# Backward attention of a decode block: dV made up to eight heads ahead of dK, and the matmuls of dq spread over the fronts

## The chip, the cores and the metric

The kernel runs on one core of a Trainium2 chip. The metric is the device time of one launch in microseconds; the number given for a kernel is the median of several runs. Five engines work side by side, each with a queue of its own that it takes in order: TensorE (PE), VectorE (DVE), ScalarE (ACT), GpSimd (POOL) and SyncE (SP). SP does no arithmetic here; it issues nearly all transfers between HBM and the memory on the chip (SBUF). The transfers themselves run on 16 DMA engines that the core's queues share.

## The reference

One layer of a decoder for one new token per sequence (batch B = 4), forward and backward. There are H = 32 heads of width Dh = 128 over a cache of Sk = 4096 positions:

```python
q = (x_ln @ wq).reshape(B, 1, H, Dh).transpose(0, 2, 1, 3)
p = softmax(einsum("bhqd,bhkd->bhqk", q, k_cache) * Dh ** -0.5)
o = einsum("bhqk,bhkd->bhqd", p, v_cache)
h = x + o.reshape(B, 1, H * Dh) @ wo
out = h + swiglu(layernorm(h), w1, w3, w2)
# returned: out, and the gradients of x, k_cache, v_cache, wq, wo, w1, w3, w2
```

All is bfloat16. For each of the 128 pairs of sequence and head, called heads here and counted by s, the backward part needs dP = V dO, dS = P (dP − c) scale with c = dO·O, and the outer products dV = P dOᵀ and dK = dS qᵀ. A head's K, V, dK or dV is 4096 × 128 values, 1024 KB. So K is read once, V twice, dK and dV are written once: 128 MB for each of the five streams.

## The kernel before, in words

The order of every engine's queue is the order in which the program writes the instructions; there is no scheduler. What an instruction waits for follows from the tiles that it reads and writes.

**Memory.** 23 slots of 8 KB per partition (class `Slot`) hold everything large: a head of K, V, dK or dV, a piece of a weight matrix, or 16 of the matrices M. `give()` puts a slot at the back of a list, and the next request takes the front of it; an instruction that writes to a slot waits until the work that last used it has ended, transfers included. V's second reading uses a ring of its own (`vring`) of seven slots once the first heads are through.

**Forward part.** It streams K and V by pairs of heads, makes the softmax and, for each head, M = Vᵀ [P K, P] on TensorE (slots `Ms`, eight of them, 16 heads each), whose columns later give dq. Then comes a middle part (the `with ExitStack() as cm` block): the gated MLP forward and backward, the gradient dh at the attention's output, and the first eight columns of heads of dO (`dO_columns(0, 8, ...)`, L907 to L940). V loads for the backward part (L797) are issued as slots come free. dV of heads 0 and 1 are made here already.

**Backward part.** Its pieces are functions:

- `front(s)` turns V of a head: four groups of eight transposes on TensorE (L764), each copied back over V by ScalarE (L765); then eight matmuls with dO as stationary operand (L1177) add dP of four heads into one PSUM tile. The stationary operand is a window of 32 columns into one of four zero-padded tiles `zd`, in which `dO_window(s)` puts the column of dO (GpSimd, L1142). `front(s)` fills the window of head s + 2. Then V's slot goes back to the ring, and `load_ahead` and `prefetch` issue the next V load into it from SP.
- `rows_out` and `rows_T` copy the finished dP of four heads out and turn it (L1152, L1159), inside the next group's first front; `group_dS` makes dS of the four heads on VectorE (L1191, L1194).
- `P_pairs(s)` lays each value of P down twice (GpSimd, L1147, three buffers); `replicate(i0)` spreads four rows of dO and of q over all partitions (TensorE L1128, ScalarE L1131).
- `grad_V(s)` and `grad_K(s)` make an outer product each on VectorE (L770) into a fresh slot, and SP stores it (L781, L1201).

Ahead of the loop, fronts 0 to 4 are written, with dV of heads 2 and 3 behind fronts 2 and 3; then `group_dS(0)`. In the loop, round s writes `front(s + 5)`, `grad_V(s + 3)`, `grad_K(s)`:

```python
        O0, S0, L, LV = 2, 21, 5, 3
```

Two generators are advanced step by step in the rounds: `rest_of_dO`, unit "o", from round 2 to 20 (the other 24 heads of dO in pages of eight, with the transposes of wo), and `side_work`, unit "s", from round 21, three steps a round for 15 rounds and two after. `side_work` begins with dq: one fp32 matmul a head (L964), three heads a step, which releases a slot of M after each 16 heads; then dx, the gradients of wq, w2, w1, w3 and wo.

Of the kernel before, what the change touches and what calls it, by code (L numbers as in the profile page):

```python
# [9 lines left out]
FP32 = mybir.dt.float32  # L10
BF16 = mybir.dt.bfloat16
# [13 lines left out]
def kernel(  # L25
# [22 lines left out]
    nc = tc.nc  # L48
    P = nc.NUM_PARTITIONS

    B = A_x.shape[0]
# [3 lines left out]
    Dh = A_k_cache.shape[3]  # L55
    F = B_w1.shape[1]
    NH = B * H
    HD = H * Dh
    assert NH == P and Dh == P and H == 32 and Sk == 32 * P
    assert D == 4 * P and F % P == 0  # L60
    DC = D // P
# [5 lines left out]
    MC = 16  # L67
# [3 lines left out]
    x2 = A_x.rearrange("b s d -> (b s) d")  # L71
# [91 lines left out]
    ident_b = const.tile([P, P], BF16, name="ident_b")  # L163
# [14 lines left out]
    def ones_window(col):  # L178
# [11 lines left out]
                          in_=rowg[:, None, :, None].to_broadcast([P, 4, 8, 4]))  # L190
# [70 lines left out]
    with ExitStack() as c0:  # L261
# [11 lines left out]
        for h in range(H):  # L273
            for cc in range(DC):
                nc.tensor.matmul(qT_ps[:, h, :], lhsT=wq_s[cc].b(HD)[:, h * Dh:(h + 1) * Dh], rhs=xhatT[:, cc, :],
                                 start=(cc == 0), stop=(cc == DC - 1))
# [4 lines left out]
        for r in range(2):  # L281
            for t_ in range(2):
                for q in range(4):
                    nc.tensor.matmul(qr_ps[32 * q:32 * (q + 1), 2 * r + t_, :], lhsT=ident_b[:, 64 * r + t_:64 * (r + 1):2],
                                     rhs=qT_bf[:], start=True, stop=True, tile_position=(0, 32 * q))
# [3 lines left out]
    Ms = []  # L289

    def M_of(s):
        return Ms[s // MC].f(MC * (Dh + 1)).rearrange("p (n c) -> p n c", c=Dh + 1)[:, s % MC, :]
# [305 lines left out]
    units = {"d": d_hh_units()}  # L598

    def step(k, n=1):  # L600
        for _ in range(n):
            next(units[k], None)
# [110 lines left out]
    pers2 = ctx.enter_context(tc.tile_pool(name="pers2", bufs=1, reuse_waits="tile"))  # L713
    O_sb = pers2.tile([NH, Dh], BF16, name="O_sb")
    dOT_bf = pers2.tile([P, NH], BF16, name="dOT_bf")
    dOT_f = pers2.tile([P, NH], FP32, name="dOT_f")
# [8 lines left out]
    dqT_bf = pers2.tile([P, NH], BF16, name="dqT_bf")  # L725
    dqr_bf = pers2.tile([NH, Dh], BF16, name="dqr_bf")

    dhT = pers2.tile([P, DC, B], BF16, name="dhT")
    dhT_f = pers2.tile([P, DC, B], FP32, name="dhT_f")


    def dO_columns(h0, h1, ps, tag):
        s0, s1 = h0 * B, h1 * B
        dOT_ps = ps.tile([P, 512], FP32, tag=tag, name="dOT_ps")
        for h in range(h0, h1):
            for jj in range(DC):
                nc.tensor.matmul(dOT_ps[:, h * B:(h + 1) * B], lhsT=wo_page(h)[:, h % 8, jj, :], rhs=dhT[:, jj, :],
                                 start=(jj == 0), stop=(jj == DC - 1))
        nc.vector.tensor_copy(out=dOT_bf[:, s0:s1], in_=dOT_ps[:, s0:s1])
        nc.vector.tensor_tensor(out=dOT_f[:, s0:s1], in0=dOT_bf[:, s0:s1], in1=OT_f[:, s0:s1], op=ALU.mult)  # L740

    def dO_rows(h0, h1, ps_, tag_):
        s0, s1 = h0 * B, h1 * B
        pq = ps_.tile([P, Dh], BF16, tag=tag_, name="pdo_rows")
        nc.tensor.transpose(pq[0:s1, :], dOT_bf[:, 0:s1], ident_b[:])
        nc.scalar.copy(out=dOrows_bf[0:s1, :], in_=pq[0:s1, :])
        c_ps = ps_.tile([P, 512], FP32, tag=tag_, name="c_ps")
        nc.tensor.matmul(c_ps[:, s0:s1], lhsT=ones_f[:], rhs=dOT_f[:, s0:s1], start=True, stop=True)
        nc.vector.tensor_copy(out=c_rep[:, s0:s1], in_=c_ps[:, s0:s1])
        nc.gpsimd.tensor_copy(out=dOT_f[:, s0:s1], in_=dOT_bf[:, s0:s1])  # L750
# [26 lines left out]
    def grad_V(s):  # L777
        b, h = bh_of(s)
        gv = Slot("gv")
        outer(gv.heads(), P2s.pop(s), reps["rdo", s // REP][:, s % REP, :])  # L780
        nc.sync.dma_start(out=rows_of(out_3[b, h]), in_=gv.heads())  # L781
        if s > 1:
            gv.give()
        else:
            first_gv.append(gv)
# [14 lines left out]
    with ExitStack() as cm:  # L800
# [108 lines left out]
        for b0, b1 in ((0, 1), (1, B)):  # L909
# [8 lines left out]
            else:  # L918
                nc.scalar.copy(out=rep_bufs["rdo"][0][:, b0:b1], in_=ps[:, b0:b1])
        dO_columns(0, 8, psC, "cols")  # L920
        mid_w["wo"][0].give()
        grad_V(1)
        V_T(0, psT, range(2, SJ // GW))
# [3 lines left out]
    with ExitStack() as c2:  # L927
# [20 lines left out]
            gu.append((dst, ps, n))  # L948


        def side_work():
            pt = psg.tile([P, Dh], BF16, tag="gps", name="pt_O")
            nc.tensor.transpose(pt[:], OT_bf[:], ident_b[:])
            nc.scalar.copy(out=O_sb[:], in_=pt[:])
            dq_ps = psx.tile([P, 512], FP32, tag="x2", name="dq_ps")
            wq2s = deque()

            def load_wq2(cc):
                if cc < DC:
                    wq2s.append(Slot("wq2"))  # L960
                    nc.sync.dma_start(out=wq2s[-1].b(HD), in_=A_wq[cc * P:(cc + 1) * P, :])

            for s in range(NH):
                nc.tensor.matmul(dq_ps[:, s:s + 1], lhsT=M_of(s)[:, 0:Dh], rhs=dOT_f[:, s:s + 1], start=True, stop=True)  # L964
                if s % MC == MC - 1:
                    Ms[s // MC].give()
                    if s // MC in (3, 5):
                        load_wq2(s // MC // 2 - 1)
                if s % 3 == 2:
                    yield  # L970
            yield
            t = rs.f(2080)[:, 1536:1536 + NH]
            nc.vector.tensor_tensor(out=t, in0=c_rep[:], in1=kPT[:], op=ALU.mult)
# [144 lines left out]
            nc.scalar.copy(out=dh, in_=dr_ps[:])  # L1118

        units["o"] = rest_of_dO()  # L1120
        def replicate(i0):
            K_ = 8 * B if i0 < 8 * B else P
            for nm_, rows in (("rdo", dOrows_bf), ("rq", qrows_bf)):
                if (nm_, i0 // REP) in reps:
                    continue
                ps = psrep.tile([P, REP, Dh], FP32, tag="rep", name="rep_ps")
                for i in range(REP):
                    nc.tensor.matmul(ps[:, i, :], lhsT=ident_b[0:K_, i0 + i:i0 + i + 1].to_broadcast([K_, P]), rhs=rows[0:K_, :],  # L1128
                                     start=True, stop=True)
                rt = rep_bufs[nm_][i0 // REP % 2]  # L1130
                nc.scalar.copy(out=rt, in_=ps[:])  # L1131
                reps[nm_, i0 // REP] = rt

        rows = {}
        dS2s = {}
        zd = [bw3.tile([P, 132], BF16, name=f"zd{i}", tag=f"zd{i}", bufs=1) for i in range(B)]
        for i in range(B):
            nc.gpsimd.memset(zd[i][:], 0.0)

        def dO_window(s):  # L1140
            if s < NH:
                nc.gpsimd.tensor_copy(out=zd[s % B][:, 32:132:67], in_=dOT_bf[:, s:s + 1].to_broadcast([P, 2]))  # L1142

        def P_pairs(s):
            if s < NH and s not in P2s:
                P2s[s] = bw3.tile([P, SJ, 2], BF16, tag="P2", name="P2")
                nc.gpsimd.tensor_copy(out=P2s[s][:], in_=P_all[:, s, :, None].to_broadcast([P, SJ, 2]))  # L1147
# [6 lines left out]
        def rows_T():  # L1154
            if "sb" in rows:
                sb = rows["t"] = rows.pop("sb")
                rows["T"] = psD.tile([P, B, P], FP32, tag="dPT", name="dPT_ps")
                for jj in range(4):
                    nc.tensor.transpose(rows["T"][:, jj, :], sb[:, jj * P:(jj + 1) * P], ident_f[:])  # L1159

        def front(s):
            hl = s % B
            if s not in VTs:
                for g in range(SJ // GW):
                    V_T(s, psT, range(g, g + 1))
                    if hl == 0 and g == 0:
                        rows_out()
                    if hl == 0 and g == 2:
                        rows_T()
            VT = VTs[s].heads()  # L1170
            if hl == 0:
                rows["acc"] = psD.tile([P, 512], FP32, tag="dP", name="dP_ps")
            dO_window(s + 2)
            for u in range(2):
                for c in range(4):
                    j0 = 8 * c + 4 * u
                    nc.tensor.matmul(rows["acc"][32 * c:32 * (c + 1), :], lhsT=zq_window(zd[hl], 2 * hl + u),  # L1177
                                     rhs=VT[:, j0:j0 + 4, :], start=(hl == 0 and u == 0),
                                     stop=(hl == B - 1 and u == 1), tile_position=(0, 32 * c))
            if hl == B - 1:  # L1180
                rows["ps"] = rows.pop("acc")
            sl = VTs.pop(s)
            (vring if len(V2s) + len(VTs) + len(vring) < NV2 else free).append(sl.i)
# [22 lines left out]
                load_V2(nc.sync)  # L1206


        O0, S0, L, LV = 2, 21, 5, 3

        def load_ahead(s):
            prefetch()
            if s < NH and s not in V2s and s not in VTs:
                load_V2(nc.sync)

        for s in range(2):
            dO_window(s)
        for s in range(L):
            load_ahead(s)
            P_pairs(s)  # L1220
            front(s)
            if s < 2:
                first_gv[s].give()
            elif s < LV + 1:
                grad_V(s)
        group_dS(0)
        for s in range(NH):
            load_ahead(s + L)
            if s % REP == 0 and s + REP < NH:
                replicate(s + REP)  # L1230
            P_pairs(s + L)
            if s + L < NH:
                front(s + L)
            elif s + L == NH:
                rows_out()
                rows_T()
            if s > 0 and s + LV < NH:
                grad_V(s + LV)
            grad_K(s)
            if s % B == B - 1 and s + 1 < NH:  # L1240
                group_dS((s + 1) // B)
            if s >= S0:
                step("s", 3 if s < S0 + 15 else 2)
            elif s >= O0:
                step("o")
        step("s", 400)


# [28 lines left out]
```

## Time and profile before

| | |
|---|---|
| median of nine runs | 1714.16 us (1712.49 to 1715.0) |
| the profiled execution | 1712.67 us |
| its span, first to last instruction | 1710.7 us |
| busy: PE, DVE, ACT, POOL | 74%, 72%, 57%, 24% of the span |
| moved | 707.50 MB, 414 GB/s in the mean |
| V load, dV store, dK store (1024 KB each), issue to landing | 19.9, 20.0, 20.1 us (medians) |
| one outer product (L770) | 2.29 us |
| one copy of eight transposes (L765) | 1.02 us |

The profile belongs to one execution. Its page gives busy time by engine, the span cut into 40 slices with the busy share of each engine and the rate of the transfers in each, the chain of work that ended last, and the costliest groups of instructions. Further views of the same trace list single instructions in order of time, with the idle time in front of each and what ended it, and busy time in any windows of the span. The forward part ends and the middle part begins near 660 us, and fronts 0 to 4 lie between 703 and 725 us. "PEclk" is the clock that TensorE was granted, as a share of full speed. The busy share of the DMA engines counts the time that packets took, so a window can show a high share and a low rate.

### The profile page before, as it was taken

The page shows a single profiled execution, that of the slowest core. Times are in us where ns is not written, and L with a number is a line of the kernel's source. Part 1 is how long each engine was busy: PE and PEld are TensorE (multiplying, and loading weights), DVE is VectorE, ACT ScalarE, POOL GpSimd, SP SyncE. Part 2 cuts the span into 40 slices and gives each one's busy share as a digit, 9 for nine tenths or more (in the row PEclk, how much of TensorE's full clock was granted, in tenths as well). Part 3 has the DMA queues.
Part 4 walks back from the last instruction along what each step waited for, and adds up shares of the span by engine and source line. Part 5 has one row for each costly group of instructions (what it writes and reads, how often), then busy time and mean ns, then how long its engine had stood idle before and what let it go on. Part 6 is the DMA issues. An engine that isn't in the chain of part 4 may idle for free. (4 is left out here: it accounts for less than half of the span.)

```text
span 1710.7 us, 38404 instructions
## 1 busy us (share of the span) xinstructions
PE 1257.9 (74%) x16180; PEld 932.1 (54%) x16180; DVE 1236.0 (72%) x1294; ACT 968.9 (57%) x1502; POOL 403.0 (24%) x680
## 2 busy tenths in 40 slices
PE   5889888888888888777788877774666665666660
PEld 4667766777677666645456755442333433444440
DVE  5989899989998996467676467765476566666672
ACT  3556444544544444677654467875567665675540
POOL 2211232223222321131212145410022222200120
PEclk8999999999999999998876689978789687786765
DMA  9999999999999999899999999999999999999996
GB/s 400 424 424 424 424 423 424 424 423 422 417 424 410 420 407 398 319 391 426 425 425 426 426 409 425 425 426 426 425 426 422 420 423 420 413 423 417 416 422 277
DMA packets 101741, 707.50 MB, mean 414 GB/s; under 512 B 11052, under 2 KB 15288, under 8 KB 17600
## 3 DMA queue, kind: packets, MB, share of 16 engines
q1 hardware_dynamic: 101152, 704.95, 99.0%
q8 instruction: 127, 2.08, 0.5%
q14 instruction: 46, 0.38, 0.1%
q0 software_dynamic: 416, 0.10, 0.0%
HBM read 422.59 MB, written 282.34 MB: 412 GB/s over the span
## 5 line engine op out<-in xcount | busy, mean ns | idle before, releaser
L765 ACT COPY V<-pt_tps 128x1024 bf16<-128x1024 bf16 x512 | 490.6, 1025 | 146.5 <-PE pt_tps L764 121.6
L764 PE MATMUL pt_tps<-ident_b,V 128*128 128x128 bf16 x4096 | 364.3, 251 | 201.0 <-ACT V L765 173.4
L764 PEld LDWEIGHTS <-V 128*128 128x128 bf16 x4096 | 312.0, 115 | 266.9 <-issue 228.7
L770 DVE TENSOR_TENSOR gv<-P,reps 128x4096 bf16<-128x4096 bf16 x125 | 286.9, 2295 | 163.7 <-DMA out_dram<-gv 112.9
L770 DVE TENSOR_TENSOR gk<-dS,reps 128x4096 bf16<-128x4096 bf16 x128 | 293.3, 2293 | 96.5 <-DMA out_dram<-gv 85.3
L421 DVE TENSOR_TENSOR PK<-Kn,PK 128x4096 bf16<-128x4096 bf16 x128 | 292.3, 2283 | 25.9 <-POOL PK L417 25.6
L436 PE MATMUL M_ps<-PK,Vn 128*128 128x130 bf16 x4096 | 286.1, 222 | 25.8 <-DMA Vn<-in_A_v_cache_dram 25.7
L436 PEld LDWEIGHTS <-Vn 128*128 128x128 bf16 x4096 | 254.9, 100 | 44.7 <-DMA Vn<-in_A_v_cache_dram 35.5
L328 DVE STREAM_TRANSPOSE KT<-Kn 128x512 f32<-128x512 f32 (+1 forms) x321 | 250.6, 797 | 0.3 <-issue 0.2
L1147 POOL COPY P<-P_all 128x64 bf16<-128x64 bf16 x127 | 113.0, 890 | 560.4 <-DVE gv L770 560.2
L1177 PE MATMUL dP_ps<-V,zd 128*32 128x512 bf16 x1024 | 183.1, 442 | 66.9 <-ACT V L765 64.2
L323 ACT COPY KT<-pt_tps 128x1024 bf16<-128x1024 bf16 x128 | 129.5, 1012 | 180.2 <-PE pt_tps L322 146.1
L334 POOL TENSOR_TENSOR W<-qrep,wmask 128x128 bf16<-128x128 bf16 x128 | 123.7, 966 | 82.7 <-PE S_ps L354 67.8
L417 POOL COPY PK<-P_all 128x64 bf16<-128x64 bf16 x128 | 32.7, 255 | 415.0 <-ACT P_all L411 411.9
L1142 POOL COPY zd<-dOT_bf 128x2 bf16<-128x2 bf16 x128 | 115.0, 899 | 62.7 <-PE dP_ps L1177 62.6
L1177 PEld LDWEIGHTS <-zd 128*32 128x32 bf16 x1024 | 37.6, 95 | 156.3 <-issue 142.1
L1131 ACT CAST reps<-rep_ps 128x512 bf16<-128x512 f32 x62 | 36.4, 586 | 128.4 <-DVE gk L770 95.3
L1191 DVE TENSOR_SCALAR dPr<-dPT_ps,c_rep 128x32 f32<-128x32 f32 x128 | 23.2, 242 | 87.5 <-PE dPT_ps L1159 87.5
L411 ACT COPY P_all<-pt_P 32x64 bf16<-32x64 bf16 x256 | 52.1, 203 | 53.4 <-PE pt_P L407 51.2
L322 PE MATMUL pt_tps<-ident_b,Kn 128*128 128x128 bf16 x1024 | 80.8, 223 | 0.0
L446 PE MATMUL kP_ps<-PK,onesw 128*32 128x512 bf16 x1024 | 79.6, 388 | 0.0
L386 ACT ACTIVATE E<-S_ps,nm 128x256 f32<-128x256 f32 x64 | 30.4, 474 | 85.7 <-DVE nm L383 85.6
(239 smaller groups left out, 1312.8 us busy)
## 6 DMA issues: line engine op xcount, KB each, us to landing
Kn<-in_A_k_cache_dram SPq DMA_DIRECT2D x128, 1024.0 KB, 15.2
Vn<-in_A_v_cache_dram SPq DMA_DIRECT2D x128, 1024.0 KB, 15.5
V<-in_A_v_cache_dram SPq DMA_DIRECT2D x128, 1024.0 KB, 19.9
out_dram<-gv SPq DMA_DIRECT2D x128, 1024.0 KB, 20.0
out_dram<-gk SPq DMA_DIRECT2D x128, 1024.0 KB, 20.1
wq<-in_A_wq_dram SPq DMA_DIRECT2D x8, 1024.0 KB, 15.7
out_dram<-gw SPq DMA_DIRECT2D x6, 896.0 KB, 19.7
wo<-in_A_wo_dram SPq DMA_DIRECT2D x4, 1024.0 KB, 11.4
```

The lines of the kernel that those rows point to most:

```text
L322: nc.tensor.transpose(pt[:, i, :], Kn[:, c * GW + i, :], ident_b[:])
L323: nc.scalar.copy(out=KT[:, c * GW:(c + 1) * GW, :], in_=pt[:])
L328: nc.vector.transpose(out=KT[:, c * w_:(c + n) * w_], in_=Kn[:, c * w_:(c + n) * w_])
L334: nc.gpsimd.tensor_tensor(out=W[:, hl], in0=qrep[:, :, s:s + 1].to_broadcast([P, 4, 32]), in1=wmask[:, hl, None, :].to_broadcast([P, 4, 32 ...
L421: nc.vector.tensor_tensor(out=PK[:, :, 0:Dh].rearrange("p j (r t) -> p j r t", t=2), in0=Ks[s].heads().rearrange("p j (r t) -> p j r t", t=2),
L436: nc.tensor.matmul(hold["M"][:], lhsT=Vn[:, j, :], rhs=PK[:, j, :], start=(j == 0), stop=(j == SJ - 1))
L764: nc.tensor.transpose(pt[:, i, :], v[:, g * GW + i, :], ident_b[:])
L765: nc.scalar.copy(out=v[:, g * GW:(g + 1) * GW, :], in_=pt[:])
L770: nc.vector.tensor_tensor(out=dst.rearrange("p j (r t) -> p j r t", t=2), in0=col2[:, :, None, :].to_broadcast([P, SJ, Dh // 2, 2]), in1=r ...
L1142: nc.gpsimd.tensor_copy(out=zd[s % B][:, 32:132:67], in_=dOT_bf[:, s:s + 1].to_broadcast([P, 2]))
L1147: nc.gpsimd.tensor_copy(out=P2s[s][:], in_=P_all[:, s, :, None].to_broadcast([P, SJ, 2]))
L1177: nc.tensor.matmul(rows["acc"][32 * c:32 * (c + 1), :], lhsT=zq_window(zd[hl], 2 * hl + u), rhs=VT[:, j0:j0 + 4, :], start=(hl == 0 and u ...
```

## The change

- dV is made ahead of dK by up to eight heads. `grad_V` is called through `more_V(upto)`. Ahead of the loop it makes dV up to head 3, 5, 6, 7 and 8 behind fronts 0 to 4. In round s it goes up to head s + 8; from round 60 the lead shrinks by one each four rounds, to three at round 76. The P copies go two heads ahead of dV.
- `replicate` is split: dO's rows for the next four heads are written after the third dV of a group, q's in each third round of four, ahead of `front`. Before, both stood at the first round of four.
- dq leaves `side_work` and becomes a unit "q" of four heads a step, advanced inside `front`, between the transposes and the matmuls with dO: two steps in fronts 1 to 4, one in fronts 13 to 36. Slots of M come free with it; the loads of wq for dx follow after the sixth and seventh slot of M. `side_work` without dq starts at round 35, two steps a round.
- The tiles `zd` move to a pool that is opened before the middle part, so their zeroing is written there, and the first four windows of dO are filled right behind the first columns of dO. `front(s)` fills window s + 2 as before, from head 4 on.

What is computed, its precision, and the bytes that are loaded and stored stay the same.

```diff
+    zd = [pers2.tile([P, 132], BF16, name=f"zd{i}") for i in range(B)]
+    for i in range(B):
+        nc.gpsimd.memset(zd[i][:], 0.0)
+
+    def dO_window(s):
+        if s < NH:
+            nc.gpsimd.tensor_copy(out=zd[s % B][:, 32:132:67], in_=dOT_bf[:, s:s + 1].to_broadcast([P, 2]))
...
         dO_columns(0, 8, psC, "cols")
+        for s in range(B):
+            dO_window(s)
         mid_w["wo"][0].give()
         grad_V(1)
...
+        def dq_work():
+            for s in range(NH):
+                assert s < rowsd["n"]
+                nc.tensor.matmul(dq_ps[:, s:s + 1], lhsT=M_of(s)[:, 0:Dh], rhs=dOT_f[:, s:s + 1], start=True, stop=True)
+                if s % MC == MC - 1:
+                    Ms[s // MC].give()
+                    if s // MC in (5, 6):
+                        load_wq2(s // MC - 5)
+                if s % 4 == 3:
+                    yield
+
+        units["q"] = dq_work()
...
-            for s in range(NH):
-                nc.tensor.matmul(dq_ps[:, s:s + 1], lhsT=M_of(s)[:, 0:Dh], rhs=dOT_f[:, s:s + 1], start=True, stop=True)
-                if s % MC == MC - 1:
-                    Ms[s // MC].give()
-                    if s // MC in (3, 5):
-                        load_wq2(s // MC // 2 - 1)
-                if s % 3 == 2:
-                    yield
...
-        zd = [bw3.tile([P, 132], BF16, name=f"zd{i}", tag=f"zd{i}", bufs=1) for i in range(B)]
-        for i in range(B):
-            nc.gpsimd.memset(zd[i][:], 0.0)
...
+        dq_at = {f: 2 for f in range(1, 5)}
+        dq_at.update({f: 1 for f in range(13, 37)})
...
-            dO_window(s + 2)
+            if s + 2 >= B:
+                dO_window(s + 2)
+            step("q", dq_at.get(s, 0))
...
-        O0, S0, L, LV = 2, 21, 5, 3
+        O0, S0, S1, L = 2, 21, 35, 5
+        gvd = {"n": 2}
+
+        def more_V(upto):
+            while gvd["n"] < min(NH, upto):
+                s = gvd["n"]
+                P_pairs(s)
+                replicate("rdo", s - s % REP)
+                grad_V(s)
+                P_pairs(s + 1)
+                P_pairs(s + 2)
+                gvd["n"] += 1
+                if s % REP == 2:
+                    replicate("rdo", s + 2)
+
+        def lead_V(s):
+            return 8 - min(5, max(0, s - 56) // 4)
...
-        for s in range(2):
-            dO_window(s)
+        for s in range(3, 6):
+            P_pairs(s)
         for s in range(L):
             load_ahead(s)
-            P_pairs(s)
             front(s)
-            if s < 2:
-                first_gv[s].give()
-            elif s < LV + 1:
-                grad_V(s)
+            if s == 0:
+                for gv in first_gv:
+                    gv.give()
+            more_V((4, 6, 7, 8, 9)[s])
+            if s == 0:
+                replicate("rdo", REP)
         group_dS(0)
         for s in range(NH):
             load_ahead(s + L)
-            if s % REP == 0 and s + REP < NH:
-                replicate(s + REP)
-            P_pairs(s + L)
+            if s % REP == 2:
+                replicate("rq", s + 2)
...
-            if s > 0 and s + LV < NH:
-                grad_V(s + LV)
+            if s > 0:
+                more_V(s + 1 + lead_V(s))
             grad_K(s)
...
-            if s >= S0:
-                step("s", 3 if s < S0 + 15 else 2)
-            elif s >= O0:
+            if O0 <= s < S0:
                 step("o")
+            if s >= S1:
+                step("s", 2)
```

More of the change, by code (lines that the diff above doesn't have):

```diff
@@ L740, in dO_columns @@
         nc.vector.tensor_tensor(out=dOT_f[:, s0:s1], in0=dOT_bf[:, s0:s1], in1=OT_f[:, s0:s1], op=ALU.mult)
+    rowsd = {"n": 0}
     def dO_rows(h0, h1, ps_, tag_):
         s0, s1 = h0 * B, h1 * B
+        rowsd["n"] = s1
         pq = ps_.tile([P, Dh], BF16, tag=tag_, name="pdo_rows")
@@ L948, in grad_unit, with load_wq2 @@
             gu.append((dst, ps, n))
+        wq2s = deque()
+        def load_wq2(cc):
+            if cc < DC:
+                wq2s.append(Slot("wq2"))
+                nc.sync.dma_start(out=wq2s[-1].b(HD), in_=A_wq[cc * P:(cc + 1) * P, :])
+        dq_ps = psx.tile([P, 512], FP32, tag="x2", name="dq_ps")
+        def dq_work():
[9 more added lines that the diff above has]
+        units["q"] = dq_work()
         def side_work():
@@ L954, in side_work @@
             nc.scalar.copy(out=O_sb[:], in_=pt[:])
[L955 to L961, printed above, removed]
-            for s in range(NH):
-                nc.tensor.matmul(dq_ps[:, s:s + 1], lhsT=M_of(s)[:, 0:Dh], rhs=dOT_f[:, s:s + 1], start=True, stop=True)
-                if s % MC == MC - 1:
-                    Ms[s // MC].give()
-                    if s // MC in (3, 5):
-                        load_wq2(s // MC // 2 - 1)
-                if s % 3 == 2:
-                    yield
             yield
@@ L1120, with replicate @@
         units["o"] = rest_of_dO()
-        def replicate(i0):
+        def replicate(nm_, i0):
+            if i0 >= NH or (nm_, i0 // REP) in reps:
+                return
             K_ = 8 * B if i0 < 8 * B else P
[L1123 to L1132, printed above, removed]
+            rows = dOrows_bf if nm_ == "rdo" else qrows_bf
+            ps = psrep.tile([P, REP, Dh], FP32, tag="rep", name="rep_ps")
+            for i in range(REP):
+                nc.tensor.matmul(ps[:, i, :], lhsT=ident_b[0:K_, i0 + i:i0 + i + 1].to_broadcast([K_, P]), rhs=rows[0:K_, :],
+                                 start=True, stop=True)
+            rt = rep_bufs[nm_][i0 // REP % 2]
+            nc.scalar.copy(out=rt, in_=ps[:])
+            reps[nm_, i0 // REP] = rt
         rows = {}
         dS2s = {}
-        zd = [bw3.tile([P, 132], BF16, name=f"zd{i}", tag=f"zd{i}", bufs=1) for i in range(B)]
-        for i in range(B):
-            nc.gpsimd.memset(zd[i][:], 0.0)
-        def dO_window(s):
-            if s < NH:
-                nc.gpsimd.tensor_copy(out=zd[s % B][:, 32:132:67], in_=dOT_bf[:, s:s + 1].to_broadcast([P, 2]))
         def P_pairs(s):
```

## Prediction

> **What bounds the kernel now.** I read the page's rows of slices and queues first, then busy time by windows around the start of the backward part, then the order of events there on VectorE, SP, GpSimd and TensorE.
>
> ```profile
> DMA  9999999999999999899999999999999999999996
> GB/s 400 424 424 424 424 423 424 424 423 422 417 424 410 420 407 398 319 391 426 425 425 426 426 409 425 425 426 426 425 426 422 420 423 420 413 423 417 416 422 277
> q1 hardware_dynamic: 101152, 704.95, 99.0%
> ```
>
> The transfers fill the span: in most slices (42.8 us each) they move 424 to 426 GB/s, while no engine is busy over 74%. The total of 707.5 MB at 425 GB/s alone is 1664.7 us, of a span of 1710.7. So only a stretch in which the transfers fall below that rate can be won back, and the one large such stretch between the ends is slices 16 and 17 (319 and 391). In windows (length, busy time of PE, PEld, DVE, ACT, POOL, then clock, share, GB/s):
>
> ```profile
> 700.00:710.00 10.00, 6.40 (x63) 4.48 (x64) 7.19 (x7) 5.31 (x7) 5.94 (x15) 0.83 0.90 373
> 710.00:720.00 10.00, 6.96 (x84) 4.30 (x81) 0.00 (x0) 7.52 (x8) 0.72 (x4) 1.00 0.40 120
> 720.00:730.00 10.00, 7.08 (x79) 4.93 (x77) 7.45 (x8) 8.37 (x11) 2.57 (x2) 0.91 0.86 302
> 730.00:740.00 10.00, 7.74 (x72) 4.86 (x69) 5.01 (x3) 6.51 (x7) 1.69 (x4) 0.75 0.97 327
> 740.00:750.00 10.00, 7.40 (x80) 4.52 (x80) 5.96 (x8) 7.54 (x10) 2.45 (x2) 1.00 1.00 419
> ```
>
> VectorE does nothing from 710 to 720 while the transfers stand at 120 GB/s. Summing what is missing to 424 GB/s in 2 us windows from 706 to 740 gives **13.2 us** of lost transfer time; 700 to 706 lacks 0.4 more. From 740 to 1140 the rate is 424 throughout. The events (start, length, engine, line; in brackets the idle time before and who ended it):
>
> ```profile
> 706.94 2.29 DVE L770 TENSOR_TENSOR gv<-P,reps 128x4096 bf16<-128x4096 bf16 x1 [0.43 <-DMA out_dram<-gv]
> 722.36 0.72 DVE L1191 TENSOR_SCALAR dPr<-dPT_ps,c_rep 128x32 f32<-128x32 f32 x4 [13.13 <-PE dPT_ps L1159]
> ...
> 700.04 6.83 SPq L781 DMA_DIRECT2D out_dram<-gv  x3
> 714.50 0.34 SPq L797 DMA_DIRECT2D V<-in_A_v_cache_dram  x1
> 714.93 0.38 SPq L781 DMA_DIRECT2D out_dram<-gv  x1
> 719.49 5.87 SPq L797 DMA_DIRECT2D V<-in_A_v_cache_dram  x2
> ...
> 704.27 2.34 POOL L1147 COPY P<-P_all 128x64 bf16<-128x64 bf16 x1
> 703.38 0.61 PE L1177 MATMUL dP_ps<-V,zd 128*32 128x512 bf16 x8 [2.52 <-POOL zd L1142]
> ```
>
> VectorE has made dV of heads 0 to 3 by 709.2 and then stands 13.1 us before the first dS, which needs four whole fronts and the transposes of the sums behind them (a front: 32 transposes of V, four ScalarE copies of 1.02 us, eight matmuls with dO). The fourth dV, ready at 709.2, is issued only at 714.93: SP takes its queue in order, and ahead of it is a V load that waits at 714.50 for the front that reads its slot. Loads follow at the pace of the fronts, some 5 us apart (matmuls of fronts ended at 704.0, 709.4, 714.4, 719.4, 724.9).
>
> **What the Trainium skill says.** "Perfetto Trace Analysis", Optimization Strategy: a kernel can have several regimes and gains by interleaving them. The trace agrees that this is such a place: four fronts without output, then outputs. "SBUF — State Buffer", Who interferes with whom: a VectorE instruction with two SBUF inputs blocks a GpSimd instruction that reads SBUF until it ends. The trace agrees: the P copy above took 2.34 us beside the dV product of 704.22 to 706.51; its median is 0.24.
>
> **The change, part by part.**
>
> *dV ahead.* Before the first dS VectorE now makes dV of heads 0 to 8 instead of 0 to 3; the stores of heads 0 to 6 stand on SP ahead of the next V load. A product takes 2.29 us. A transfer of 1024 KB takes 1.049 MB / 424 GB/s = 2.47 us of the transfer engines, so VectorE alone can nearly feed them. No byte is added: dV leads dK by 8 heads up to head 56, then shrinks to 3 by head 76, the lead that it has now, so I cost the end at nothing: the same last loads, outputs and drain remain.
>
> *Slots.* Following allocation through the code, dV 2 takes the slot of V 0 (free after front 0), dV 3 that of dV 0's store (landed at 706.9 in the trace), then dV 4, 5 and 6 rotate over the slots of dV 1, 2 and 3, dV 7 takes V 1's, dV 8 dV 4's. The shortest store here landed 5.2 us after issue; three slots with 2.3 + 5.2 us each still give one store per 2.5 us, about the transfer rate.
>
> *dq.* 8 heads in each of fronts 1 to 4, 4 heads in each of fronts 13 to 36, instead of about 9 per head of the loop from head 21. The rows of today give 11 records in 1.37 us, two records a head: 0.25 us a head. Eight heads are 2.0 us, behind the last transposes and ahead of the dO matmuls. In front 2 of today the transposes end at 712.6 and the last ScalarE copy at 713.8, then five matmuls run to 714.4. With dq the eight matmuls start at 714.6 and end at 715.5: **+1.1 us a front**, four times. It releases two slots of M before front 5; output then circulates over six slots instead of four. The later share is 1.0 us per head in a stretch where a head takes 7.4 us (three transfers); today PE carries 2.2 us of dq per head from 880 to 1000 without any loss of rate. Hidden.
>
> *zd.* The zeroing (four of 0.2 us) leaves the place between dO's cast and the first window, and the first copies move up. Front 0 waited 2.5 us for it. Its last ScalarE copy ends at 701.3, so it could start then (gain 2.0 us); but at 700.25 VectorE begins the product of dV 1 and holds the copies to 702.5, as the SBUF page says, unless GpSimd comes first (gain 0.7). I take 0.7; the range has both.
>
> *Replication.* The same 62 copies, dO's and q's now apart. Two of dO (0.6 us of ScalarE each) come inside fronts 1 and 3: +1.2 us. Today such copies idle ScalarE 95 us in all behind a dK just issued; now they come later than the product they wait for. ScalarE isn't late after 740: nothing.
>
> *Added waits.* P copies go out two heads ahead, so on GpSimd the window for front 4 stands behind P 6 and P 7, which wait for dV 3 and dV 4 (711.6 at the latest, 713.9 if blocked by a product). Front 4 needs it about 728. In the loop the window of front s+8 stands behind P of s+10, which waits for dV of s+7, four rounds earlier (today three): nothing. dq in front 13 waits for the cast of dO's second page, one round old; SP, V loads and stores would wait behind PE there, but only some 2 us, and stores then land 20 us after issue (queue 8 deep): covered. Without that queue it would cost those 2 us.
>
> *The sum.* I carry the times through. Fronts end: 0 at 703.3, 1 at 710.3 (copy 0.6, dq 1.1), 2 at 716.4, 3 at 723.1, 4 at 729.8, 5 at 734.8. dV 2 is made by 705.8, dV 3 by 709.2 (slot), 4 by 711.5, 5 by 713.8, 6 by 716.5, 7 by 718.8, 8 by 721.1. The first dS comes at 726, 3.7 us later than now, first dK out at 730. Laid end to end at 2.47 us on the transfer engines, with 1.3 us from ready to first bytes (0.2 to issue; the load issued alone at 714.50 left 714 to 716 at a share of 0.21, so its packets start some 1.1 us later): dV 0, 1 end at 706.5 as now; gap 0.5; dV 2 to 709.5; gap 1.0; dV 3, 4, 5, 6, V 9, dV 7, V 10, dV 8 follow without a gap to 730; V 11 (issued 729.8): gap 1.2; dK 0, then V 12, dV 9, dK 1 at 735: three transfers for each 5 us front, so no gap after. Gaps 2.7 us. There is one unknown: where a load joins a short queue today the rate stays near 250 GB/s for some 4 us though the share is 0.9 (716 to 720, 726 to 730). If the queue of two that I find is deep enough this costs nothing; if each of two such joins costs 4 us × 0.41 it is 3.3. I take 1.7. Recovered: 13.2 + 0.4 − 2.7 − 1.7 = **9.2 us**; with the low ends (late stores, both joins, no zd gain, some blocked P copies) about 5; with everything filled 13.6.
>
> The profiled execution took 1712.67 us (1.97 beyond its span). 1712.67 − 9.2 = 1703.5. It is 1.5 us below the median of the nine runs, 1714.16, so in the median I expect **1705.0 us**; a full fill would be 1700.6, a recovery of 5 us 1709.2.
>
> **The rivals.** A measurement of this kernel can tell about 0.2%, 3.4 us, from no change.
>
> *Half filled.* Short queues stay slow, as between 726 and 738 today (221 to 299 GB/s with two or three transfers out), and the later dS opens a second hole from 726 to 736. If 10 us more run at 270 instead of 424 GB/s, 3.6 us more are lost: recovery 5 or less, 1709 to 1713. For it: those windows. Against it: stores alone run at 397 (708 to 710).
>
> *No effect.* The queue fills, but what is won is given back as the lead shrinks between heads 56 and 76, or at the end, where the last fronts set the pace: 1714. Against it: loads and stores are full at 424 up to 1690, and the last load lands 20 us after its issue, in a queue that will be as deep.
>
> *Slower.* Output and loads share HBM, and the rate isn't the same everywhere: 1460 to 1480 has 410 GB/s and 1560 to 1580 413, at full share. The place is 740 to 1140, with dV eight heads on instead of three. At 410 instead of 424 it takes 400 × 14/410 = 13.7 us more: 1705.0 + 13.7 = 1718.7. From about 415 on it eats the 9 us. For it: the slow windows have no cause I can see. Against it: from 1140 to 1300 the same three streams keep 426.
>
> **How the numbers follow.** Forecast (recovery 5 to 13.6) 0.78; half filled 0.10, of which 0.06 gains more than 3.4 us; no effect 0.06; slower 0.06. Faster: 0.78 + 0.06 = 0.84; within: 0.04 + 0.06 = 0.10; slower 0.06. The range starts at a full fill, 1700.6, and reaches through the better part of half filled, to 1711.0; above lie 0.16, below some 0.03 for a shift of the whole level.
>
> **What would show it.** Right: 710 to 720 at 350 GB/s or more with five VectorE products in it; 700 to 740 lacking 3 to 8 us instead of 13.6; first dS near 726; dq in fronts 1 to 4 with no dO matmul over 1.5 us later for it; 740 to 1140 still at 424. Wrong: a gap of over 3 us between 721 and 735 (dS too late), V 9 issued after 720, the window copies ending a wait of front 4, or a rate under 420 after 740.

## The result, and the profile after

| | before | changed |
|---|---|---|
| median | 1714.44 us (29 runs, 1712.12 to 1718.47) | 1705.87 us (9 runs, 1704.76 to 1706.99) |
| ratio to before | | 0.995, 95% interval 0.9942 to 0.9958 |
| profiled execution, span | 1712.67, 1710.7 us | 1706.06, 1704.1 us |

The change saves 8.6 us, where 9.2 were forecast. The page's row of the slices' transfer rates, then the windows around the start of the backward part (the same columns as those of before: length, busy time of PE, PEld, DVE, ACT, POOL, clock, share, GB/s):

```profile
GB/s 400 424 425 424 424 424 424 423 423 424 415 423 412 421 404 401 378 393 425 425 425 425 426 424 426 426 426 426 423 420 420 420 416 416 422 424 412 417 423 276
```

```profile
700.00:710.00 10.00, 7.86 (x86) 6.27 (x83) 8.51 (x8) 6.25 (x9) 3.62 (x9) 0.66 0.92 381
710.00:720.00 10.00, 9.71 (x83) 8.08 (x84) 8.22 (x4) 4.27 (x5) 2.27 (x5) 0.65 0.92 384
720.00:730.00 10.00, 8.80 (x97) 7.77 (x97) 3.88 (x7) 7.78 (x10) 3.28 (x4) 0.83 1.03 324
730.00:740.00 10.00, 7.54 (x94) 5.52 (x93) 9.97 (x6) 7.07 (x9) 5.48 (x4) 1.00 0.96 342
740.00:750.00 10.00, 7.21 (x84) 4.35 (x82) 5.78 (x3) 7.99 (x10) 5.54 (x5) 1.00 1.01 424
```

Slice 16 rises from 319 to 378 GB/s, and the window of 710 to 720 from 120 to 384: VectorE works there for 8.2 us instead of none. Summed over 2 us windows from 700 to 760, each counted by its shortfall from 424 GB/s, 6.3 us of transfer time are now lacking, where 13.6 were. Most of what is left, 4.4 us, lies from 720 to 738. Two columns of the window before it, 710 to 720, point to a reason: TensorE is busy for 9.7 of 10 us there, and its granted clock is 0.65 where it was 1.00. The events on VectorE, SP, GpSimd and TensorE (start, length; in brackets the idle time before and who ended it):

```profile
709.75 2.29 DVE L781 TENSOR_TENSOR gv<-P,reps 128x4096 bf16<-128x4096 bf16 x1 [0.19 <-DMA out_dram<-gv]
712.40 2.29 DVE L781 TENSOR_TENSOR gv<-P,reps 128x4096 bf16<-128x4096 bf16 x1 [0.36 <-POOL P L1158]
716.12 6.88 DVE L781 TENSOR_TENSOR gv<-P,reps 128x4096 bf16<-128x4096 bf16 x3 [1.42 <-DMA out_dram<-gv]
728.99 0.73 DVE L1207 TENSOR_SCALAR dPr<-dPT_ps,c_rep 128x32 f32<-128x32 f32 x4 [5.99 <-PE dPT_ps L1170]
...
701.14 17.62 SPq L792 DMA_DIRECT2D out_dram<-gv  x7
719.75 0.34 SPq L808 DMA_DIRECT2D V<-in_A_v_cache_dram  x1
720.64 0.57 SPq L792 DMA_DIRECT2D out_dram<-gv  x1
726.12 0.34 SPq L808 DMA_DIRECT2D V<-in_A_v_cache_dram  x1
...
701.35 2.71 POOL L734 COPY zd<-dOT_bf 128x2 bf16<-128x2 bf16 x4 [3.61 <-DVE dOT_bf L747]
703.75 1.04 PE L1193 MATMUL dP_ps<-V,zd 128*32 128x512 bf16 x8 [1.78 <-POOL zd L734]
709.16 3.52 PE L976 MATMUL dq_ps<-dOT_f,M 128*128 128x1 f32 x16
717.22 1.90 PE L976 MATMUL dq_ps<-dOT_f,M 128*128 128x1 f32 x16
723.43 2.06 PE L976 MATMUL dq_ps<-dOT_f,M 128*128 128x1 f32 x16
```

The wait before the first dS has shrunk from 13.1 to 6.0 us, because dV 4 to 8 are now made in it. But dS itself comes at 729.0 instead of 722.4. In front 1 the eight heads of dq took 3.52 us, at half the speed of the next (1.90). V 9 leaves at 719.75 (before: 714.50), V 10 at 726.12; from 720 to 726 the rates are 352, 250 and 270 GB/s.

### The profile page after: what moved, and what is told of

Its sections match the earlier page's. It is cut to its first block, busy times and chain, and to the rows that moved or that the text cites. A ratio compares the mean times of both kernels' runs of the same rounds, so it can differ in the third digit from the quotient of the medians.

```text
span 1704.1 us, 38404 instructions
## 1 busy us (share of the span) xinstructions
PE 1247.3 (73%) x16180; PEld 925.9 (54%) x16180; DVE 1237.1 (73%) x1294; ACT 967.5 (57%) x1502; POOL 389.8 (23%) x678
## 4 chain that ended last, share of the span: by engine, by line
DMA 48%; PE 6%; ACT 5%; DVE 2%; issue 1%; DVEq 0%; POOL 0%; SPq 0%; ACTq 0%
DMA out_dram<-gk 17%; DMA V<-in_A_v_cache_dram 16%; DMA out_dram<-gv 14%; ACT V L776 4%; PE pt_tps L775 1%; PE dP_ps L1193 1%; DVE gv L781 1%; PE M_ps L436 1%; PE dq_ps L976 1%; DVE PK L421 1%; PE pt_w L565 0%; DVE gk L781 0%; PE pt_wo L574 0%; ACT Pn L400 0%; PE kP_ps L446 0%
## 5 line engine op out<-in xcount | busy, mean ns | idle before, releaser
L775 PE MATMUL pt_tps<-ident_b,V 128*128 128x128 bf16 x4096 | 360.6, 249 | 208.0 <-ACT V L776 150.9
L775 PEld LDWEIGHTS <-V 128*128 128x128 bf16 x4096 | 307.1, 114 | 286.5 <-issue 206.4
L1193 PE MATMUL dP_ps<-V,zd 128*32 128x512 bf16 x1024 | 172.1, 443 | 53.8 <-ACT V L776 50.6
L1158 POOL COPY P<-P_all 128x64 bf16<-128x64 bf16 x125 | 84.2, 674 | 495.3 <-DVE gv L781 495.2
L734 POOL COPY zd<-dOT_bf 128x2 bf16<-128x2 bf16 x128 | 132.3, 1035 | 132.2 <-PE dP_ps L1193 128.5
L322 PEld LDWEIGHTS <-Kn 128*128 128x128 bf16 x1024 | 62.0, 100 | 25.9 <-issue 25.8
L354 PE MATMUL S_ps<-KT,W 128*32 128x256 bf16 x1536 | 75.2, 285 | 0.5 <-DVE KT L328 0.2
## 6 DMA issues: line engine op xcount, KB each, us to landing
V<-in_A_v_cache_dram SPq DMA_DIRECT2D x128, 1024.0 KB, 19.9
```

The lines of the kernel that those rows point to most:

```text
L322: nc.tensor.transpose(pt[:, i, :], Kn[:, c * GW + i, :], ident_b[:])
L775: nc.tensor.transpose(pt[:, i, :], v[:, g * GW + i, :], ident_b[:])
```

## The experiments

The comparisons below rest on the same reading: the median of the runs, and the transfer time lacking from 700 to 760 in the kernel's own profile. A profile is of one execution, which can lie some us off the median. Where a kernel's code differs from the changed kernel, the edit is shown; "..." marks lines left out.

**dV alone.** From the changed kernel, dq goes back to the side work with its old rounds, and zd back to its old place:

```diff
-        for s in range(B):
-            dO_window(s)
...
-        units["q"] = dq_work()
...
+            for s in range(NH):
+                nc.tensor.matmul(dq_ps[:, s:s + 1], lhsT=M_of(s)[:, 0:Dh], rhs=dOT_f[:, s:s + 1], start=True, stop=True)
...
-            step("q", dq_at.get(s, 0))
...
+        for s in range(2):
+            dO_window(s)
```

> The change with dq back in the side work from round 21 and the zd tiles back in their old place: only dV ahead (with the split replication). My theory: nearly all of the gain is the dV products in the hole, and dq in fronts 1 to 4 delays dS and the V loads by several us, so this alone gains as much as the whole change or more: 8 to 11 us under the kernel before (1703 to 1706). Rival (dV needs the two slots of M and the early window to be of use): 3 to 6 us only, 1708 to 1711.

Measured: 1703.61 us (before on this chip 1713.80; ratio 0.9942, 0.9929 to 0.9954), with 3.6 us lacking. The products alone bring 10.2 us, as my theory had it; neither the slots of M nor the early windows are needed for it. The interval overlaps that of the changed kernel (0.9942 to 0.9958), so this pair does not show that dV alone is faster than the whole change.

**dq alone.** The other half: the kernel before, with only dq moved into the fronts, and the side work without dq from round 35.

```diff
+        units["q"] = dq_work()
...
+        dq_at = {f: 2 for f in range(1, 5)}
+        dq_at.update({f: 1 for f in range(13, 37)})
...
+            step("q", dq_at.get(s, 0))
```

> The kernel before with dq alone moved into the fronts (eight heads in fronts 1 to 4, four in fronts 13 to 36), dV where it was. My theory: dq lengthens fronts 1 to 4 by 1 to 3 us each with no dV to fill the time, so the hole before the first dS grows: 3 to 7 us slower than the kernel before (1717 to 1721). Rival (dq is hidden behind ScalarE's copies and its slots help): within 1 us of before.

Measured: 1719.15 us, ratio 1.0031 (1.0019 to 1.0042): 5.4 us slower than before. Its windows:

```profile
700.00:710.00 10.00, 7.10 (x94) 5.71 (x93) 7.83 (x7) 5.02 (x7) 5.57 (x13) 0.67 0.83 342
710.00:720.00 10.00, 9.71 (x80) 8.56 (x81) 1.23 (x1) 5.24 (x6) 0.36 (x2) 0.63 0.22 89
720.00:730.00 10.00, 8.80 (x98) 7.35 (x99) 0.48 (x3) 6.64 (x8) 0.71 (x4) 0.83 0.80 256
730.00:740.00 10.00, 8.51 (x94) 6.50 (x91) 9.36 (x7) 6.65 (x9) 3.39 (x3) 0.83 0.77 247
```

The same TensorE columns as in the changed kernel (busy 9.71 and 8.80, clock 0.63 and 0.83) without dV beside them: VectorE idle for 18 us, 19.9 us lacking.

**The windows of zd.** The changed kernel, with zd zeroed and filled in the old place.

```diff
-        for s in range(B):
-            dO_window(s)
...
-            if s + 2 >= B:
-                dO_window(s + 2)
+            dO_window(s + 2)
...
+        for s in range(2):
+            dO_window(s)
```

> The change with the zeroing and the first windows of zd in their old place. In the trace the early windows ended at 704.06, held by the product of dV 1, so they saved front 0 well under 1 us. My theory: 0 to 1 us slower than the changed kernel. Rival (early windows are a main part of the gain, the full wait of 2.5 us): 2 to 3 us slower than the changed kernel.

Measured: 1703.52 us, ratio 0.9944 (0.9931 to 0.9956), which is not told apart from the changed kernel's 0.995, and 7.2 us lacking in the profile, which is of the slowest of its five runs (1706.53). In the trace the part works: front 0's matmuls begin 3.5 us after the cast of dO instead of 2.7. That 0.7 us does not show in the time. The rival is out.

**dq from front 5 on.**

```diff
-        dq_at = {f: 2 for f in range(1, 5)}
-        dq_at.update({f: 1 for f in range(13, 37)})
+        dq_at = {f: 1 for f in range(5, 37)}
```

> The change with dq as four heads a front from front 5 to 36, none in fronts 1 to 4. My theory: fronts 1 to 4 become 1 to 3 us shorter each, first dS near 723 instead of 729, V 9 some 4 us earlier; the hole of 6.3 us shrinks to 2 or 3: 2 to 4 us faster than the changed kernel (1702 to 1704). Rival (the slots of M released early are what keeps the stores going, or the hole is bounded by VectorE's slots): no faster than the changed kernel, or 1 to 3 us slower.

Measured: 1702.41 us, ratio 0.9937 (0.9923 to 0.9951), 2.6 us lacking. Its windows, and below its first dS and V loads:

```profile
700.00:710.00 10.00, 7.75 (x75) 5.33 (x72) 8.50 (x8) 6.34 (x8) 3.61 (x9) 0.66 0.93 387
710.00:720.00 10.00, 7.27 (x84) 4.54 (x84) 9.77 (x5) 7.72 (x10) 8.17 (x6) 1.00 1.01 412
720.00:730.00 10.00, 7.00 (x85) 4.86 (x84) 6.88 (x9) 7.49 (x10) 4.53 (x5) 1.00 0.99 365
730.00:740.00 10.00, 7.96 (x99) 5.91 (x99) 4.88 (x3) 7.76 (x10) 0.83 (x4) 1.00 1.01 424
```

```profile
724.12 0.73 DVE L1206 TENSOR_SCALAR dPr<-dPT_ps,c_rep 128x32 f32<-128x32 f32 x4 [3.05 <-PE dPT_ps L1170]
...
717.09 0.56 SPq L808 DMA_DIRECT2D V<-in_A_v_cache_dram  x1
721.23 0.34 SPq L808 DMA_DIRECT2D V<-in_A_v_cache_dram  x1
```

dS is 4.9 us earlier than in the changed kernel, V 9 2.7 and V 10 4.9 us, VectorE is busy throughout from 710 to 720, and the rate is full from 730 on. The slots of M, free later here, are not missed.

**The changed kernel again**, on one chip with the next two.

> The changed kernel once more, for a comparison on one chip with the others of this group: 1703 to 1707, its windows of 700 to 760 lacking 6 to 7 us of transfer time.

Measured: 1705.77 us, ratio 0.9947 (0.9935 to 0.996); 5.0 us lacking in this profile, 1 us less than I expected. It is of the fastest of six runs (1703.25).

**Fewer dV ahead.** From the kernel with dq from front 5 on:

```diff
-            return 8 - min(5, max(0, s - 56) // 4)
+            return 5 - min(2, max(0, s - 56) // 4)
...
-            more_V((4, 6, 7, 8, 9)[s])
+            more_V((4, 5, 6, 6, 6)[s])
```

> dq from front 5 on, as in e4, but only six dV instead of nine ahead of the first dS and a lead of five heads, not eight, in the loop. My theory: what counts is the number of dV products that lie in the hole; three fewer take 3 x 2.47 = 7.4 us of transfers out of it, of which some 1.5 come back with loads issued earlier: 5 to 7 us slower than e4 (1707 to 1710), and the windows of 700 to 760 lack 8 to 9 us instead of 2.8. Rival (the gain is the depth of the lead in the loop, or the hole needs only two more dV): less than 3 us slower than e4.

Measured: 1706.12 us, ratio 0.9957 (0.9943 to 0.9971), 7.6 us lacking. It is 3.7 us above the kernel with nine, in medians of two groups, between both expectations; in the profiles 5.0 more are lacking and the span is 4.4 longer. So the number of products in the hole does count. The lead in the loop was shortened with it, but the span has grown by no more than the stretch from 700 to 760 lost, so the loop has no visible part in it. I had priced the products too high: with six stores on SP instead of seven, V 9 leaves 2.6 us earlier (714.46), and of the 7.4 us taken out 2.4 came back, where I had allowed 1.5.

**Ten dV ahead**, and the first window by VectorE, from the same kernel:

```diff
+        if h0 == 0:
+            nc.vector.tensor_copy(out=zd[0][:, 32:132:67], in_=dOT_bf[:, 0:1].to_broadcast([P, 2]))
...
-        for s in range(B):
+        for s in range(1, B):
             dO_window(s)
...
-            return 8 - min(5, max(0, s - 56) // 4)
+            return 9 - min(6, max(0, s - 56) // 4)
...
-            more_V((4, 6, 7, 8, 9)[s])
+            more_V((4, 6, 7, 8, 10)[s])
```

> e4 (dq from front 5 on) with ten dV ahead of the first dS and a lead of nine, and the first window of dO copied by VectorE right behind dO itself, ahead of the product of dV 1, so that front 0 need not wait for GpSimd. My theory: of the 2.8 us that e4 still lacks, the tenth store covers about 1 and the earlier front 0 about 0.7: 0.5 to 2 us faster than e4 (1700 to 1702). Rival (VectorE stands 3 us before dS in e4 and the tenth product fills that, but its store waits on SP behind a load): no change from e4 within 1 us.

Measured: 1702.73 us, ratio 0.9933 (0.9921 to 0.9946), 2.7 us lacking. Front 0 starts 0.9 us after the cast instead of 2.7, the tenth product fills VectorE up to dS (idle before it: none instead of 3.1 us), and the time stays. My expectation fell, the rival's number held, though not for its reason: the tenth product ended at 724.0 and its store left ahead of the next load (725.37). Between 720 and 730 the kernel still lacks 1.8 us.

**The kernel before, a second profile.**

> The kernel before, for a second profile. In the changed kernel and in three partial versions the middle part ended 0.8 to 1.1 us later than in the first profile of before, although that part is the same in some of them. If this is chance, this profile has dO's cast near 701, not 699.9, and a loss of transfer rate of 1.2 to 1.5 us from 694 to 700; if the versions bring it about, it repeats 699.9.

Measured: 1713.92 us. The cast of dO stands at 701.13, 1.2 us are lacking from 694 to 700, and 14.9 from 700 to 760, with a span of 1712.0. So it is chance, as far as one more profile can tell: the first profile of before had reached the backward part about 1 us early.

**Three on one chip**: dq from front 5 on once more, then only the first 32 heads of dq moved by four fronts, then the changed kernel a third time.

```diff
-        dq_at = {f: 2 for f in range(1, 5)}
+        dq_at = {f: 2 for f in range(5, 9)}
```

> e4 once more (dq as four heads a front from front 5 on), beside the changed kernel on one chip. If the 3.4 us between them in separate groups are real, 2 to 4.5 us under the changed kernel of this group, with 2 to 3.5 us lacking from 700 to 760; if they were chance, within 1.5 us of it.

> The change with its first 32 heads of dq moved by four fronts: eight heads in each of fronts 5 to 8 and none in fronts 1 to 4, the rest as in the change. My theory: it is the place that costs, ahead of the first dS, not eight heads a front: as fast as e9 within 1.5 us. Rival (eight heads in one front overload TensorE or slow its clock wherever they stand): as slow as the changed kernel, 3 us above e9.

> The changed kernel, as the partner of e9 and e10 on this chip: 1704 to 1707, 5 to 6.5 us lacking from 700 to 760.

Measured: 1702.22 us (ratio 0.9928, 0.9915 to 0.9941), 1702.35 us (0.993, 0.9918 to 0.9942) and 1705.42 us (0.9945, 0.993 to 0.9959); 2.6, 2.8 and 7.3 us lacking (for the last I had expected 5 to 6.5). The changed kernel has 1705.4 to 1705.9 in three groups, dq from front 5 on 1702.2 and 1702.4 in two: some 3 us between them. And eight heads a front cost nothing that can be seen when they stand behind the first dS: the two kernels are 0.13 us apart. There too one block of dq ran at half speed (in front 7), as in each of the three profiles of the changed kernel (in front 1, 1 and 3). TensorE's list and a window of that kernel:

```profile
743.77 3.51 PE L976 MATMUL dq_ps<-dOT_f,M 128*128 128x1 f32 x16
753.63 1.90 PE L976 MATMUL dq_ps<-dOT_f,M 128*128 128x1 f32 x16
```

```profile
740.00:750.00 10.00, 9.75 (x73) 8.48 (x74) 6.79 (x3) 5.22 (x7) 0.36 (x2) 0.50 1.01 423
```

At a clock of 0.50 and with TensorE busy for 9.75 of 10 us, the transfers stay at 423 GB/s. That a queue which is already deep covers it is my reading; the depth was not varied.

**One account for all of them.** Span less the time lacking from 700 to 760:

| kernel | lacking | span | difference |
|---|---|---|---|
| before, two profiles | 13.6, 14.9 | 1710.7, 1712.0 | 1697.1, 1697.1 |
| changed, three profiles | 6.3, 5.0, 7.3 | 1704.1, 1701.3, 1704.2 | 1697.8, 1696.3, 1696.9 |
| dV alone | 3.6 | 1701.7 | 1698.1 |
| dq alone | 19.9 | 1717.4 | 1697.5 |
| zd late | 7.2 | 1704.6 | 1697.4 |
| dq from front 5, two profiles | 2.6, 2.6 | 1699.8, 1700.6 | 1697.2, 1698.0 |
| six dV ahead | 7.6 | 1704.2 | 1696.6 |
| ten dV ahead | 2.7 | 1700.9 | 1698.2 |
| 32 heads of dq in fronts 5 to 8 | 2.8 | 1701.6 | 1698.8 |

The spans differ by 17.6 us, what is left by 2.5. So each of these edits acts through the rate in this stretch and hardly anywhere else.

## Why the prediction was right, point by point

- **What bounds the kernel, and the hole.** Right. The transfers do, and only the hole could be refilled; the table above shows it for kernels on both sides.
- **dV ahead.** Right, and at least the whole of the gain: alone it brings 10.2 us. The walk through the slots held for dV 2 to 5: counted from the cast of dO, they came at most 0.4 us later and 0.8 us earlier than it said. dV 6 started at 716.1, 0.8 us after the walk's time; it waited for the landing of dV 3's store. That leaves a gap from 718 to 720 (225 GB/s, 0.9 us lost) which the walk did not have; the gap that I had put at 709 did not come (410 GB/s there).
- **dq: the term that was mis-sized.** I put "+1.1 us a front" on it, from the last ScalarE copy of a front and dO matmuls of 1.0 us behind dq. At full clock it is less: in front 2 of the changed kernel the copy ends at 718.7, dq at 719.1 and the eight matmuls, in 0.6 us, at 719.7, some 0.3 us later than without dq; in front 3 it is 0.7.

  What I left out is the granted clock. In each of the six profiles with eight heads a front, one block ran at half speed: in front 1 of the changed kernel the copy ends at 710.4 and the matmuls at 713.65, 2.6 us later than they could. The three fronts ahead of dS add up to 3.6 us for my 3.3, and the slow clock holds other work up as well. From the cast of dO to the first dS it took 28.0, 26.8 and 29.4 us in the three profiles, 23.3 with dq moved back, where the walk had 26. So dq puts the first dS off by 3.5 to 6.1 us, not by 3.3.

  The Trainium skill has the two rates in "TensorE: Matmul & The Clock Gate", What's actually happening: a gate that lets all pulses or half of them through, set by how busy the array has been. 3.52 against 1.90 us and the clock of 0.50 agree with that. The page lowers the clock after idle time; here it stayed at 0.50 from 703.3 to 716.9 while TensorE was busy for 12.6 of 13.6 us. The fall itself is not dq's: with dq from front 5 on, the clock is 0.50 from 703.1 to 709.9 as well (the windows of 700 to 710 have 0.66 in both kernels), but then it is back at 1.00. Why it stays low for longer beside dq was not tried.
- **The short queue: about the size I gave it; the hole behind a late dS was mis-sized.** I had 1.7 us for loads that join a short queue and 1.2 for the gap ahead of V 11. From 720 to 738 the changed kernel lacks 4.4, 3.6 and 5.0 us in its three profiles. The five profiles with nine or ten dV ahead and no dq in fronts 1 to 4 lack 1.4 to 1.8 us there, nearly all of it before 730, at rates down to 242 GB/s with shares of 0.92 and more. That is about the size I gave to the short queue. The rest, some 3 us, goes away when dq alone is moved, so it comes with dq, which puts off dS and the V loads. It is the same step again.
- **zd.** Right: 0.7 us earlier, because the copies were held by the product of dV 1, as the Trainium skill has it in "SBUF — State Buffer", Who interferes with whom (2.71 us for four copies of 0.2). No gain from it shows in the time. Nor does a start 1.8 us earlier, in the kernel with ten dV ahead: there the dip from 706 to 708 is filled (451 GB/s, 266 with nine ahead), but 2.7 us in all are lacking, and 2.6 with nine.
- **Slots, replication, waits of the later dq.** Right: from 760 to 1660 both kernels lose the same, within 1 us (3.1 to 3.9 us in their five profiles), and the rate from 740 to 1140 is 425, where it was 424. The slower rival, a lower rate in that stretch, has nothing left to stand on.
- **The sum.** Recovered in the profiles: 13.6 − 6.3 = 7.3 us for the forecast 9.2. Part of the missing 1.9 is the first profile of before, which was early by about 1 us; against the second one it is 14.9 − 6.3 = 8.6. By the medians 8.6. That 8.6 lies so near 9.2 is partly luck: by the second profile the hole was 1.3 us larger than I had summed, and 1.9 us more than I forecast were left in it. The rival "half filled" named what is left, a short slow queue and a second hole behind a late dS, and its 3.6 us for that hole are near the 3 measured. But it forecast a recovery of 5 or less (its own figures give 9.2 − 3.6 = 5.6).
- **The signs.** 710 to 720 ran at 384 GB/s (350 or more forecast), 700 to 740 lacked 6.3 us (3 to 8), the rate after 740 held, and V 9 left at 719.75, just before 720. Three were missed: four products of VectorE, not five, lie wholly or in part in 710 to 720; the first dS came at 729.0, not near 726 (1.1 us of that is a later start of the backward part); and the dO matmuls of front 1 came 2.6 us later, not at most 1.5. "A gap of over 3 us between 721 and 735" left open whose gap it is: VectorE stood for 6.0 us, the transfers at no time (238 GB/s in the slowest 2 us).

A version beats both kernels: with dq from front 5 on, 1702.2 to 1702.4 us. Filling VectorE further, with a tenth dV, adds nothing that shows.

## What to carry to other kernels

Where transfers bound a kernel, add up what the rate lacks in a stage; that sum is an estimate of the most that a reordering can win there, and here it priced each variant afterwards to within 2.5 us. Fill such a hole with work that needs nothing from the late chain, and keep work that could wait (here dq) out of that chain: the changed kernel gave back about 3 of 12 us to a side task put four fronts too early. Behind the first dS, where the transfers ran at their full rate, the same task cost nothing that could be seen, even at half the clock.

## What the runs showed of the hardware that I had not expected

- Eight fp32 heads of dq in one go ran now at 1.90 us, now at 3.5 us, with the clock at 0.50 in a window where TensorE was busy for 9.75 of 10 us; which block it hit changed from profile to profile of one kernel.
- The granted clock was 1.00 or 0.50, apart from windows in which it changed. From 692 to 780 us, in half-microsecond windows of all thirteen profiles, each stretch at 0.50 lasted 3.4, 6.8, 10.2 or 13.7 us, multiples of 3.41. Each of the six profiles with eight heads of dq in a front has one stretch of 10.2 or 13.7 us, with the slow block of dq in it; in the seven others none is longer than 6.8. So the long stretch goes with dq, and moved with it to front 7; by which mechanism was not tried.
- With few transfers out, packets can fill the DMA engines' time (share 0.93 to 1.04 from 720 to 726) while only 250 to 352 GB/s move; the rate, not the share, shows such a hole.
